# Fourth score column ahead of the second K, and a later copy of q, in a fused attention and mixture-of-experts kernel

## Chip, cores and metric

The kernel runs on one core of one Trainium2 chip. The metric is the device time of one launch in microseconds (us); lower is better. The time before is 945.1 us, the median of three runs (941.18 to 945.74).

## What is computed

Three layers follow one another. The attention has 8 batches, 8 heads, 576 rows and head size 64; K and V are first averaged over groups of 8 rows, so each head has 72 keys. Two layers of experts follow (4608 tokens of width 512, 8 experts, hidden width 1024). In the first, each token goes to the expert with the largest logit and is scaled by that expert's probability; the second does the same for tokens whose skip score is positive.

```python
k_p = k.reshape(B, H, Sp, 8, D).mean(axis=3); v_p = v.reshape(B, H, Sp, 8, D).mean(axis=3)
attn = softmax(scale * q @ k_p.T);  x = attn @ v_p          # [B*S, H*D] after a transpose
e = argmax(x @ w_gate + bias[modality]);  out[t] = p[t, e] * (relu(x[t] @ w1[e]) @ w2[e])
```

## The kernel before, in words

The order of instructions on each engine is written out by hand; each engine works through its own queue in that order, and a wait holds up all that stands behind it on the same queue. The attention goes through 36 *columns* of 128 query rows (all 8 heads at once), in the loop at L562, which runs to 39 because the product with V (`emit_AV`) trails the scores by LAG = 3 columns. A *unit* is 256 rows of one batch (two columns) or the last 64 rows of two batches (one column). Columns 0 to 3 belong to batch 0 and columns 4 to 7 to batch 1; column 8 has the rest of both. Columns 9 to 17, 18 to 26 and 27 to 35 are the next three pairs of batches.

One column goes through these steps:

- `split_q` (L156): ScalarE rearranges a loaded q unit; `emit_qT` (L283): TensorE transposes it into `ps_q`, ScalarE copies it out.
- `emit_S` (L305): eight matmuls against the pooled K (`KB`), VectorE takes the maximum (`mx`, L316); then VectorE runs what has been put off in the list `late` (L319), and five ticks of the background work are issued.
- `emit_exp` (L332): TensorE subtracts the maximum in PSUM (L336), ScalarE takes the exponential (L340). `ps_s` has one buffer, so the scores of a column wait for the exponential of the one before.
- `emit_eT` (L348) one column later, `emit_AV` (L366) three columns later, then VectorE divides by the sum (L395 to L402) and adds up the router's logits (L406).

K and V are pooled from raw loads by `pool_kb` (K of batches 0 and 1), `pool_k` (later K, in tiles of 108 rows) and `pool_v`, on GpSimd or VectorE as `pool_at` (L430) says; VectorE's share goes to `late` and so runs in the next column. `prep_kb`, `prep_k`, `prep_v1` and `prep_v2`, placed by `prep_at` (L441), transpose the pooled K and V on TensorE through the single PSUM buffer `ps_m` and copy them into `KB` and `VB`. All loads are issued on SyncE's queue: `next_q` (L481) loads q units in order, `next_kv` (L472) the K and V loads in the order of `order` (L462), each not before the column that frees its buffer.

Routing runs in the background while the attention goes on. `Background.tick` (L678) advances a generator by `pace` steps; each column has six ticks. `route` (L826) picks the expert of nine columns, counts tokens with a scan (L867), keeps the running count in `carry` (L871) and ranks tokens with two matmuls into `R` (L882, L883), which take `ps_m` as well. It is started after columns 12, 21 and 30 (`route_at`, L561); `lag` (L622) is the number of empty steps ahead of the second maximum (L850) and of the scan. `count` (L916) copies `carry` to `cb` (L919) and sums it by a matmul (L923); `early_pick` and `early_fill` call it with `copy=True`. `route_places` (L905) builds one-hot tiles `OB` on GpSimd. `early_slots` then names the tokens of the first blocks, which are gathered by GpSimd. `prepare_first` (L1488) splits the first expert's weights (`w1h`, `w1l`) and, at columns 32 and 33, transposes the first block's tokens through `ps_m` (`xT`, L1357), whose low half `xl` VectorE computes as a `late` item one column on.

The first block's products are mixed into the last columns; from about 210 us on the expert blocks run, a dense row of matmuls.

Of the kernel before, what the change touches and what calls it, by code (L numbers as in the profile page):

```python
# [55 lines left out]
def attention(tc, g, q, k, v, mid, w_gate, bias, const, moe):  # L56
# [3 lines left out]
    nc = tc.nc  # L60
    with ExitStack() as ctx:
# [28 lines left out]
        cols = []  # L90
# [9 lines left out]
        NC = len(cols)  # L100
# [322 lines left out]
        def idle():  # L423
            for _ in range(3):
# [5 lines left out]
        pool_at = {0: [(pool_kb, 1, 2, 4, P), (pool_kb, 1, 0, 2, V), (pool_kb, 1, 4, 5, V)],  # L430
                   1: [(pool_v, 1, 0, P)]}
# [5 lines left out]
        for b, cs in ((1, (3, 4, 4)), (2, (5, 6, 7)), (3, (10, 11, 12)), (4, (14, 15, 16)),  # L437
                      (5, (18, 19, 20)), (6, (20, 21, 22)), (7, (24, 25, 26))):
            for i, c in enumerate(cs):
                pool_at.setdefault(c, []).append((pool_v, b, 1, V, i, i + 1))  # L440
        prep_at = {1: [(prep_v1, 0)], 2: [(prep_kb, 1), (prep_v2, 0)],  # L441
                   5: [(prep_v1, 1)], 6: [(prep_v2, 1)], 7: [(prep_k, 0)],
                   8: [(prep_v1, 2, P)], 9: [(prep_v2, 2)], 11: [(prep_k, 1)],
                   13: [(prep_v1, 3, P)], 14: [(prep_v2, 3)],
                   17: [(prep_v1, 4)], 18: [(prep_v2, 4)], 20: [(prep_k, 2)],
                   21: [(prep_v1, 5)], 22: [(prep_v2, 5)], 24: [(prep_v1, 6)], 25: [(prep_k, 3)],
# [34 lines left out]
        def next_q(n):  # L481
            while n_q[0] < min(n, len(units)):
                load_q(n_q[0])
                n_q[0] += 1
# [77 lines left out]
        for c in range(NC + LAG):  # L562
            if c < NC:
                next_q(cols[c][0] + (5 if c > 1 else 4))
                next_kv(c)
                next_q(cols[c][0] + 5)
            bg.pace = {22: 2, 32: 1, 34: 2, 36: 3}.get(c, bg.pace)
            if 4 <= c < NC - 1:
                emit_S(c, lambda: emit_qT(c + 2))
            elif c < 4:  # L570
                if c > 0:
                    emit_S(c)
                    emit_eT(c - 1)
                    emit_exp(c)
                emit_qT(c + 2)
            elif c == NC - 1:
                emit_S(c)
                moe.gemm1_early()
# [11 lines left out]
            if c >= NC:  # L590
                for _ in av_t.pop(c - LAG - 1, ()):
                    pass
            emit_AV(c - LAG)
            if c == NC:
                emit_eT(c - 1)
                ks.close()
                moe.open_third()
            ahead = c + (3 if c < 2 else 4)
            if ahead < NC and cols[ahead][0] not in qs_t:
                split_q(cols[ahead][0])  # L600
# [19 lines left out]
            if c in route_at:  # L620
                c0, n = route_at[c]
                eng, lag = (nc.vector, (0, 0)) if c0 == 18 else (nc.gpsimd, (5, 8) if c0 == 0 else (4, 12))  # L622
# [44 lines left out]
class Background:  # L667


    def __init__(self):  # L670
        self.q = []
        self.hold = False
        self.pace = 1
# [152 lines left out]
def route(tc, g, r, lg, mask, c0, n, sp, pp, eng, wait=1, then=(), lag=(0, 0)):  # L826
# [30 lines left out]
    if n > 2:  # L857
# [13 lines left out]
        V.tensor_copy(r.carry, I[:, :, n - 1])  # L871
# [44 lines left out]
def count(tc, g, r, sp, pp, wait, copy=False):  # L916
    nc = tc.nc
    cb = sp.tile([128, E], BF16, tag="rc_cb", name="rc_cb", bufs=1)
    nc.vector.tensor_copy(cb, r.carry)  # L919
    for _ in range(wait):  # L920
        yield
    N = pp.tile([128, E], F32, tag="m", name="R")
    nc.tensor.matmul(N, lhsT=g.ones, rhs=cb, start=True, stop=True)  # L923
    if copy:
        ps, N = N, sp.tile([128, E], F32, tag="rc_N", name="rc_N", bufs=1)
        nc.scalar.copy(N, ps)
    else:
        g.bg.hold = True
    for _ in range(wait):
        yield  # L930
    return N
# [248 lines left out]
class Moe:  # L1180
# [307 lines left out]
    def prepare_first(self, c, sm, ps_q, ps_m, late):  # L1488
# [3 lines left out]
        if c in (32, 33):  # L1492
            self.g.bg.settle()
            self.xT(0, c - 32, ps_m.tile([128, 4, 128], F32, tag="m", name="ps_x"), late)
        if c == 36:
            self.gates1(0, sm)
# [598 lines left out]
```

## Time and profile before

| | us |
|---|---|
| median of three runs | 945.1 |
| the profiled execution | 943.7 |
| its span, first to last instruction | 941.9 |
| TensorE busy in the span | 893.1 (95%) |
| VectorE / ScalarE / GpSimd busy | 704.7 / 367.8 / 511.9 |

The profile is of one execution. A group of rows names the engine, the line of the kernel, the operation, the tile that is written and the tiles that are read; in a timeline a bracket gives how long the engine sat idle before the row and what released it. PEclk is the TensorE clock that was granted, as a share of 2.4 GHz.

### The profile page before, as it was taken

How to read it: one execution, taken by the hardware profiler on the slowest of the kernel's cores; microseconds unless marked ns; L12 is line 12 of the kernel's file. 1: busy time of each engine (PE TensorE's matmuls, PEld its weight loads, DVE VectorE, ACT ScalarE, POOL GpSimd, SP SyncE). 2: the span in 40 equal slices, each digit the busy share in tenths (PEclk: the TensorE clock that was granted, in tenths of full speed). 3: DMA queues.
4: the chain of work that ended last, by engine and by line, in shares of the span. 5: the costliest groups of instructions: out<-in, count | busy, mean ns of one | idle time of the engine just before them, and what ended most of it. 6: DMA issues, size and time to landing. Idle time of an engine off the chain costs nothing. (4 is left out here: it accounts for less than half of the span.)

```text
span 941.9 us, 19066 instructions
## 1 busy us (share of the span) xinstructions
PE 893.1 (95%) x6231; PEld 803.2 (85%) x6231; DVE 704.7 (75%) x1816; ACT 367.8 (39%) x727; POOL 511.9 (54%) x762
## 2 busy tenths in 40 slices
PE   7899989899999999998999989999999999999995
PEld 6799889888899999987999869999888988979993
DVE  5467886787777888889877898777665777688663
ACT  3466656453222222251222422213413556565551
POOL 5766797303246647666766556575653443445442
PEclk9999999999999999999999999999989999999998
DMA  9999965513212211441224521227115673671341
GB/s 233 216 255 264 256 195 157 193 62 121 69 58 86 74 38 64 143 153 66 83 83 130 172 79 64 75 72 253 58 65 156 206 230 126 202 244 36 111 161 44
DMA packets 86141, 126.07 MB, mean 134 GB/s; under 512 B 13192, under 2 KB 50104, under 8 KB 85866
## 3 DMA queue, kind: packets, MB, share of 16 engines
q1 hardware_dynamic: 75386, 96.68, 33.4%
q0 software_dynamic: 10608, 27.67, 9.7%
q8 instruction: 63, 1.03, 0.5%
q14 instruction: 84, 0.69, 0.2%
HBM read 182.09 MB, written 39.50 MB: 235 GB/s over the span
## 5 line engine op out<-in xcount | busy, mean ns | idle before, releaser
L1413 PE MATMUL ps_g<-xh,w1h 128*128 128x256 f32 x896 | 256.4, 286 | 2.5 <-DVE o L1652 1.5
L1413 PE MATMUL ps_g<-xl,w1h 128*128 128x256 f32 x896 | 253.3, 283 | 2.2 <-DVE xl L1366 2.2
L1413 PE MATMUL ps_g<-xh,w1l 128*128 128x256 f32 x896 | 252.7, 282 | 0.0
L1743 DVE CUSTOM_DVE_ANT_0 hr<-x,W 128x512 bf16<-128x512 f32 x324 | 228.1, 704 | 19.1 <-DVEq L1342 6.3
L1462 PE MATMUL ps_g<-w2h,hh 128*128 128x512 f32 x464 | 190.6, 411 | 3.0 <-ACT w2h L1353 1.6
L1462 PE MATMUL ps_g<-w2h,hl 128*128 128x512 f32 x464 | 185.4, 400 | 6.2 <-DVE hl L1418 6.1
L1462 PE MATMUL ps_g<-w2l,hh 128*128 128x512 f32 x464 | 184.6, 398 | 0.0
L1413 PEld LDWEIGHTS ps_g<-xh,w1h 128*128 128x128 f32 x896 | 169.7, 189 | 7.2 <-issue 2.3
L1413 PEld LDWEIGHTS ps_g<-xl,w1h 128*128 128x128 f32 x896 | 169.2, 189 | 4.0 <-DVE xl L1366 3.0
L1413 PEld LDWEIGHTS ps_g<-xh,w1l 128*128 128x128 f32 x896 | 169.5, 189 | 0.0
L1417 ACT ACTIVATE hh<-ps_g 128x512 fp32r<-128x512 f32 (+1 forms) x116 | 67.7, 584 | 248.8 <-PE ps_g L1413 246.6
L1418 DVE SCALAR_TENSOR_TENSOR hl<-ps_g,hh 128x512 fp32r<-128x512 f32 (+1 forms) x116 | 77.5, 668 | 64.1 <-ACT hh L1417 40.0
L911 POOL TENSOR_SCALAR OB<-iota,BB,pay 128x128 bf16<-128x128 bf16 x126 | 111.7, 894 | 21.5 <-DVE BB L899 21.4
L1462 PEld LDWEIGHTS ps_g<-w2h,hl 128*128 128x128 f32 x464 | 88.2, 190 | 29.5 <-DVE hl L1418 7.7
L1462 PEld LDWEIGHTS ps_g<-w2h,hh 128*128 128x128 f32 x464 | 88.6, 191 | 21.4 <-issue 2.5
L1462 PEld LDWEIGHTS ps_g<-w2l,hh 128*128 128x128 f32 x464 | 88.5, 191 | 16.7
L1354 DVE TENSOR_TENSOR w2l<-w2r,w2h 128x512 fp32r<-128x512 f32 x112 | 75.3, 710 | 6.6 <-ACT w2h L1353 4.6
L1333 POOL TENSOR_TENSOR w1l<-w1r,w1h 128x512 fp32r<-128x512 f32 x35 | 45.3, 1314 | 59.7 <-ACT w1h L1330 59.4
L1709 POOL DMA_INDIRECT out_dram<-x,dsi x38 | 47.6, 1252 | 44.5 <-DMA out_dram<-x,dsi 16.8
L1353 ACT CAST w2h<-w2r 128x512 fp32r<-128x512 f32 x112 | 63.9, 617 | 0.0
L1330 ACT CAST w1h<-w1r 128x512 fp32r<-128x512 f32 x112 | 63.7, 620 | 0.5 <-ACT hh L1417 0.5
L1323 POOL DMA_INDIRECT xg<-xd,gidx x38 | 44.1, 1162 | 33.7 <-DVE rs_lo L1174 16.5
(298 smaller groups left out, 1399.9 us busy)
## 6 DMA issues: line engine op xcount, KB each, us to landing
w1r<-in_moe_w_dram SPq DMA_DIRECT2D x128, 512.0 KB
w2r<-in_moe_w_dram SPq DMA_DIRECT2D x124, 512.0 KB
x2s<-x SPq DMA_DIRECT2D x19, 522.0 KB
v<-in_v_dram SPq DMA_DIRECT2D x48, 192.0 KB
xd<-x SPq DMA_DIRECT2D x16, 520.0 KB
q_sb<-in_q_dram SPq DMA_DIRECT2D x16, 512.0 KB
kt<-in_k_dram SPq DMA_DIRECT2D x32, 144.0 KB
x2s<-OBx SPq DMA_DIRECT2D x16, 261.0 KB
```

Of the source, the lines that this page charges most:

```text
L911: e.tensor_scalar(g.ob(c)[:, i, :], g.iota, r.BB[:, c:c + 1], r.pay[:, i, c:c + 1], ALU.is_equal, ALU.mult)
L1323: self.nc.gpsimd.indirect_dma_start(out=self.xg[i % 2][:, t, 0:w], out_offset=None, in_=src, in_offset=bass.IndirectOffsetOnAxis(ap=gidx[: ...
L1330: self.nc.scalar.copy(self.w1h[f], raw)
L1333: low() if late is None else late.append(low)
L1353: self.nc.scalar.copy(self.w2h[f], raw)
L1354: (eng or self.nc.vector).tensor_tensor(self.w2l[f], raw, self.w2h[f].bitcast(F32), ALU.subtract)
L1413: nc.tensor.matmul(out, lhsT=a[f][:, k, :], rhs=b[:, k, :], start=(n == 0), stop=(n == 11))
L1417: nc.scalar.activation(out=hh, in_=whole, func=ACTF.Relu)
L1418: nc.vector.scalar_tensor_tensor(hl, in0=whole, scalar=0.0, in1=hh.bitcast(F32), op0=ALU.max, op1=ALU.subtract)
L1462: nc.tensor.matmul(ps, lhsT=a[f][:, tt], rhs=b[f], start=(n == 0), stop=(n == 23))
L1709: self.nc.gpsimd.indirect_dma_start(out=self.out, out_offset=bass.IndirectOffsetOnAxis(ap=self.dsi[i % 2][:, t:t + 1], axis=0), in_=self.x ...
L1743: self.nc.vector.tensor_tensor_reduce(out=self.junk, in0=self.x2[i % 2][:, t, 0:DM], in1=self.W9[:, e, :], scale=1.0, scalar=0.0, op0=ALU. ...
```

## The change

The second K's last pooled part goes to column 1, its transposes (`prep_kb(1)`) from column 2 to the end of column 3's exponential, so that the scores of column 3 are issued ahead of it. `prep_v2(0)` moves forward between column 2's `emit_eT` and `emit_exp`. The first loads of q are interleaved one by one with the K and V loads, and `split_q` runs three columns ahead throughout. The V of batch 2 (the third) is pooled by VectorE and prepared one column later. `prep_k(3)` moves from column 25 to column 26. In the routing, the empty steps before the scans shrink from (5, 8) to (5, 1) and change from (4, 12) to (6, 3), the carry is copied on the engine of that route (GpSimd for the first two), `cb` is copied by ScalarE where `copy` is set, the pace rises and falls one column earlier, and the last early count waits, by `shut`, until column 35.

```diff
-        pool_at = {0: [(pool_kb, 1, 2, 4, P), (pool_kb, 1, 0, 2, V), (pool_kb, 1, 4, 5, V)],
-                   1: [(pool_v, 1, 0, P)]}
+        pool_at = {0: [(pool_kb, 1, 2, 4, P), (pool_kb, 1, 0, 2, V)],
+                   1: [(pool_v, 1, 0, P), (pool_kb, 1, 4, 5, V)]}
...
-        for b, cs in ((1, (3, 4, 4)), (2, (5, 6, 7)), (3, (10, 11, 12)), (4, (14, 15, 16)),
+        for b, cs in ((1, (3, 4, 4)), (2, (6, 7, 8)), (3, (10, 11, 12)), (4, (14, 15, 16)),
...
-        prep_at = {1: [(prep_v1, 0)], 2: [(prep_kb, 1), (prep_v2, 0)],
+        prep_at = {1: [(prep_v1, 0)],
                    5: [(prep_v1, 1)], 6: [(prep_v2, 1)], 7: [(prep_k, 0)],
-                   8: [(prep_v1, 2, P)], 9: [(prep_v2, 2)], 11: [(prep_k, 1)],
+                   9: [(prep_v1, 2, P)], 10: [(prep_v2, 2)], 11: [(prep_k, 1)],
...
-                   21: [(prep_v1, 5)], 22: [(prep_v2, 5)], 24: [(prep_v1, 6)], 25: [(prep_k, 3)],
+                   21: [(prep_v1, 5)], 22: [(prep_v2, 5)], 24: [(prep_v1, 6)],
...
         for c in range(NC + LAG):
-            if c < NC:
-                next_q(cols[c][0] + (5 if c > 1 else 4))
+            if c == 0:
+                for n in (4, 5, 6):
+                    next_q(n)
+                    next_kv(0, 1)
+                next_kv(0)
+            elif c == 2:
                 next_kv(c)
+                next_q(7)
+            elif c < NC:
                 next_q(cols[c][0] + 5)
-            bg.pace = {22: 2, 32: 1, 34: 2, 36: 3}.get(c, bg.pace)
+                next_kv(c)
+            bg.pace = {22: 2, 31: 1, 33: 2, 36: 3}.get(c, bg.pace)
+            if c == 35:
+                bg.shut = False
...
-            elif c < 4:
+            elif c < 2:
                 if c > 0:
                     emit_S(c)
                     emit_eT(c - 1)
                     emit_exp(c)
                 emit_qT(c + 2)
+            elif c == 2:
+                emit_S(c)
+                emit_eT(c - 1)
+                prep_v2(0)
+                emit_exp(c)
+                split_q(2)
+            elif c == 3:
+                emit_S(c)
+                emit_eT(c - 1)
+                emit_qT(4)
+                emit_exp(c)
+                prep_kb(1)
...
+            if c == 26:
+                prep_k(3)
             emit_AV(c - LAG)
+            if c == 3:
+                emit_qT(5)
...
-            ahead = c + (3 if c < 2 else 4)
-            if ahead < NC and cols[ahead][0] not in qs_t:
+            ahead = c + 3
+            if ahead < NC and c > 2 and cols[ahead][0] not in qs_t:
...
-                eng, lag = (nc.vector, (0, 0)) if c0 == 18 else (nc.gpsimd, (5, 8) if c0 == 0 else (4, 12))
+                eng, lag = (nc.vector, (0, 0)) if c0 == 18 else (nc.gpsimd, (5, 1) if c0 == 0 else (6, 3))
...
-        self.hold = False
+        self.hold = self.shut = False
...
-        V.tensor_copy(r.carry, I[:, :, n - 1])
+        eng.tensor_copy(r.carry, I[:, :, n - 1])
...
 def count(tc, g, r, sp, pp, wait, copy=False):
...
-    nc.vector.tensor_copy(cb, r.carry)
+    (nc.scalar.copy if copy else nc.vector.tensor_copy)(cb, r.carry)
     for _ in range(wait):
+        yield
+    while g.bg.shut:
         yield
...
             self.xT(0, c - 32, ps_m.tile([128, 4, 128], F32, tag="m", name="ps_x"), late)
+            self.g.bg.shut = True
```

## Rows read from the trace of the kernel before

**Rows 1.** Busy by stretch: us, PE, PEld, DVE, ACT, POOL, PEclk, DMA, GB/s.

```profile
30.00:40.00 10.00, 8.43 (x56) 8.02 (x56) 2.80 (x8) 3.89 (x10) 5.00 (x5) 0.83 0.83 210
...
60.00:70.00 10.00, 10.00 (x88) 9.98 (x86) 8.28 (x23) 6.96 (x15) 8.41 (x6) 1.00 1.07 298
...
330.00:353.00 23.00, 23.00 (x152) 20.74 (x151) 18.54 (x57) 4.67 (x9) 11.08 (x25) 1.00 0.08 29
```

**Rows 2.** Timeline of TensorE, columns 2 to 8: start us, us, engine, line, operation.

```profile
21.42 1.17 PE L310 MATMUL ps_s<-KB,qt 128*128 128x144 f32 x8
...
26.65 0.27 PE L217 MATMUL ps_k<-ident,kb 126*64 126x126 f32 x1
...
28.88 0.29 PE L222 MATMUL ps_k<-ident,kb 72*64 72x72 f32 x2
31.57 1.07 PE L274 MATMUL ps_g<-WGV,vt 128*96 128x32 f32 x6 [2.40 <-ACT KB L231]
32.45 2.27 PE L310 MATMUL ps_s<-KB,qt 128*128 128x144 f32 x8
...
37.85 1.14 PE L310 MATMUL ps_s<-KB,qt 128*128 128x144 f32 x8
...
41.88 1.14 PE L310 MATMUL ps_s<-KB,qt 128*128 128x144 f32 x8
...
52.22 2.29 PE L310 MATMUL ps_s<-KB,qt 128*128 128x144 f32 x8 [1.03 <-ACT ec L340]
...
58.25 1.20 PE L310 MATMUL ps_s<-KB,qt 128*64 128x144 f32 x16
```

**Rows 3.** Timeline of ScalarE: copies of q that waited, and an exponential.

```profile
27.00 0.65 ACT L340 ACTIVATE ec<-ps_s 128x576 f32<-128x576 f32 x1
...
29.66 1.04 ACT L167 COPY qs<-q_sb 128x1024 f32<-128x1024 f32 x1 [1.54 <-DMA q_sb<-in_q_dram]
...
49.10 1.05 ACT L167 COPY qs<-q_sb 128x1024 f32<-128x1024 f32 x1 [2.66 <-DMA q_sb<-in_q_dram]
```

**Rows 4.** Timeline of VectorE: maximum, V's pooling, the routing and its waits.

```profile
23.50 0.75 DVE L316 TENSOR_REDUCE mx<-ps_s 128x8 fp32r<-128x576 f32 x1
...
49.64 1.06 DVE L176 TENSOR_REDUCE v<-v 96x64 f32<-96x512 f32 x1 [0.66 <-DMA v<-in_v_dram]
...
95.04 2.37 DVE L867 TENSOR_TENSOR_SCAN rt_i<-within,rt_ms 128x72 bf16<-128x72 f32 x1
...
121.52 0.94 DVE L260 TENSOR_TENSOR VB<-v,half 96x768 f32<-96x768 f32 x1
...
129.00 0.23 DVE L850 TENSOR_REDUCE rt_my<-rt_eq 128x9 f32<-128x72 f32 x1 [1.90 <-POOL rt_eq L844]
...
169.72 0.31 DVE L867 TENSOR_TENSOR_SCAN rt_i<-within,rt_ms 128x72 bf16<-128x72 f32 x1
```

**Rows 5.** Timeline of GpSimd: K's pooling at the scan, and the one-hot tiles.

```profile
94.88 2.36 POOL L181 TENSOR_TENSOR t<-kt 108x1024 f32<-108x1024 f32 x1
...
120.91 6.86 POOL L911 TENSOR_SCALAR OB<-iota,BB,pay 128x128 bf16<-128x128 bf16 x8
```

**Rows 6.** Timeline of TensorE, columns 17 to 35.

```profile
100.50 0.51 PE L336 MATMUL ps_s<-mx,nident 128*128 128x288 f32 x2 [1.93 <-DVE mx L316]
...
119.64 1.17 PE L310 MATMUL ps_s<-KB,qt 128*128 128x144 f32 x8
...
140.36 0.40 PE L239 MATMUL ps_k<-ident,k 108*128 108x108 f32 x2 [1.62 <-POOL k L183]
...
146.88 1.23 PE L310 MATMUL ps_s<-KB,qt 128*128 128x144 f32 x8
...
164.83 1.23 PE L310 MATMUL ps_s<-KB,qt 128*128 128x144 f32 x8
...
182.01 0.19 PE L923 MATMUL R<-rc_cb,ones 128*128 128x8 bf16 x1 [2.18 <-DVE xl L320]
...
186.15 1.20 PE L310 MATMUL ps_s<-KB,qt 128*64 128x144 f32 x16
```

## Prediction

> **What bounds the kernel now.** I read the table of busy time by stretch first. The expert blocks after 210 us keep TensorE busy for all of their time at full clock, with the DMA engines nearly idle [rows 1], and the change touches nothing there: what the attention loses or saves passes one to one to the end. Second, TensorE's timeline through the attention. It runs through the columns at about 4.0 us each (37.85 to 41.88 [rows 2]) except where a wait opens a gap, so the question is which gaps close and which new ones open. A gap can cost more than itself: behind the 2.40 us before 31.57 the scores of column 3 took 2.27 us where column 4's took 1.14, and column 7's, behind 1.03 us of idle, took 2.29 [rows 2]. The granted clock of the stretch from 30 to 40 is 0.83 [rows 1], that is, part of it at 1.2 in place of 2.4 GHz. Third, the timelines of ScalarE, VectorE and GpSimd at each gap, to see what the releaser itself waited for.
>
> **Columns 2 to 8: minus 7.8 us.** Before, ScalarE stands until 29.66 for the q of columns 6 and 7 [rows 3]. The copies of the second K into `KB` are queued behind that wait, and TensorE stands 2.40 us for them; column 3, which needs neither, starts its scores at 32.45 [rows 2]. After the change column 3 needs only column 2's exponential. Column 2's scores, at 21.42 for 1.17 [rows 2], end at 22.6; with the last part of K out of the way the maximum (0.75 [rows 4]) follows at once and not at 23.50, then the subtraction (0.51 [rows 6]) and the exponential (0.65 [rows 3]); with some 0.4 for hand-overs column 3 starts at about 25.1. From there to column 4's scores TensorE does one column (4.0), the second K's transposes (26.65 to 29.17, 2.5 [rows 2]) and one more transpose of q (0.5): 32.1, not 37.85. `KB` is filled beside the product with V. The q of columns 6 and 7 is copied only after that, so column 4 gets 0.9 on top of its 4.0, and column 5 starts at 37.0, not 41.88.
> The next wait, ScalarE for q until 49.10 [rows 3], delayed column 6's exponential and so column 7's scores. It goes: that copy is issued a column later and its load ahead of half a K tile. Columns 5 and 6 with their prep matmuls take 8.7, so column 7 starts at 45.7, not 52.22; its half-clock stretch goes too, and with 4.0 and the transposes of `prep_k(0)` column 8 starts at 50.4, not 58.25. I keep 6 and 8 as bounds. `prep_v2(0)` and `prep_v1(2)` cost nothing more: the same matmuls at another place.
>
> **The loads: plus 1.5 us.** On SyncE's queue a unit of q now passes each of three K loads. Up to the third batch's V the bytes are the same, so I expect that V at 49.64 as before [rows 4]; VectorE asks for it at about 47.7 (column 7) and stands 1.9 us, of which its slack leaves some 0.3 on TensorE. The DMA engines are busy all through 60 to 70 us [rows 1], so the later loads can't come much sooner either, while their readers come eight microseconds sooner, less the one column of 4.0 by which the copies of q now come later. Waits like the one of 2.66 [rows 3] are possible, or none. I take 1.5 in all, bounds 0 and 3.
>
> **Columns 12 to 18: minus 2.2 us.** The first route's scan started at 95.04, just as GpSimd had begun a 2.36 us step of K's pooling [rows 5], and took 2.37; the same scan takes 0.31 at 169.72 [rows 4]. Column 17's maximum came late by it, and TensorE stood 1.93 us [rows 6]. Seven steps fewer put the scan into column 15, ahead of the pooling, and the carry goes to GpSimd. I add 0.3 for the slower columns around it. Bounds 1 and 2.2.
> The one-hot tiles now start a column earlier and run beside VectorE's scaling of V. VectorE's scaling at 121.52 took 0.94 us [rows 4] in the midst of eight one-hot steps of 6.86 us together [rows 5]: no delay, so I charge none. The Trainium skill, "SBUF — State Buffer", section "SBUF: two separate sides", has VectorE's instructions with two SBUF inputs and GpSimd's reads share a port under an exclusive lock held for a whole instruction. By that rule such a scaling would wait for the one-hot step in flight, up to 0.9 us, and the gain would be that much smaller where TensorE waits; the scan at 95.04 agrees with the rule, the scaling at 121.52 doesn't.
>
> **Columns 22 to 27: minus 1.4 us.** Column 22's scores to column 27's took 27.2 us (119.64 to 146.88 [rows 6]), against an estimated 21.4 without waits (five columns at 4.0 and 1.4 of prep matmuls). VectorE stood 1.90 us for GpSimd [rows 4], which was behind with one-hot tiles, and TensorE 1.62 us for K's pooling [rows 6]. These 5.8 us go with the earlier route and `prep_k(3)` a column later. New waits take their place. At pace 2 the six empty steps fall between two VectorE instructions of one column, 22, so the second maximum still waits for GpSimd and column 23's maximum is about 1.0 us late. In column 23 the copy to `cb` stands in ScalarE's queue ahead of that column's copies and exponential; it waits for GpSimd's carry, which waits for VectorE's scan, itself behind the maximum, V's third part and the logits. Column 24's scores, which need that exponential, come 1.7 us late. In column 25 the ranking falls together with the scaling of V and a third of V's pooling, some 6 us of VectorE's work in a 4 us column: 1.7 us on column 26, near the 1.93 of [rows 6]. Together 4.4 new against 5.8 old. Bounds: minus 5.8 (all hidden) and plus 2 (new half-clock stretches).
>
> **Columns 31 to 35: minus 2.1 us.** They took 21.3 us (164.83 to 186.15 [rows 6]). The count's matmul stood 2.18 us for `xl`, as VectorE still had to read `ps_m`, and a half-clock stretch followed. With `shut` it comes in column 35, free of both (3.5); the lower pace of column 31 gives 1.0. But by my count of ticks the ranking matmuls move from column 32 to column 33, behind the first `xT`, where `ps_m` is held by column 33's `xl`: the same wait in another place, about 1.7. Net 2.8, less 0.7 for the chance of a half-clock stretch. Bounds 0.3 and 3.5.
>
> **The tail: 0.** The last early count comes three of its own steps later, so its gather goes out about one early product (1.9 us) later, which is about its readers' slack. Bounds minus 0.5 and plus 1.5. `cb` on ScalarE costs nothing there: its carry is old by then.
>
> **Sum.** -7.8 + 1.5 - 2.2 - 1.4 - 2.1 = -12.0 us. The profiled execution's 943.7 (span 941.9 and 1.8 around it) would become 931.7; it lies 1.4 below the median of 945.1, so a median of the new kernel should be about 933.
>
> **The rivals.**
> *The loads take it back.* For it: the DMA share of 1.07 [rows 1]; against: no engine stands for a load of q or V after 49.64 [rows 3, 4]. Each load comes when it came before, and the columns gain only the closed half-clock stretches and the routing: about 7 us, 938.
> *The routing's new waits eat what they free.* Columns 22 to 35 give nothing or lose 2: 936.5 to 939. The ticks I counted speak for it; against, that K's pooling no longer meets the scan.
> *Nothing shows.* Columns 2 to 8 gain 4, the loads cost 3, the rest cancels but for 1: about 943.
> *Slower: GpSimd's pooling of K becomes the bound.* TensorE has stood for it before (1.62 [rows 6]). If the next K tile is not pooled when column 11 ends, at about 67, every later column waits for it, one to one. The 0.75 MB of q put ahead of K is 3.6 us at the 210 GB/s of [rows 1]; it decides once K is over 12 us late, which takes a blocked queue as well: 948 to 952.
> That an edit doesn't do what it says I see only for `cb` of the last count of all, where `copy` is not set and VectorE keeps it; nothing hangs on that.
>
> **How the numbers follow.** Forecast 0.58; loads 0.16; routing 0.15; nothing 0.07; slower 0.04. About 0.5% (4.7 us) is what a measurement of this kernel can tell from no change, so faster means below 940.4: the forecast, the loads and the routing lie there but for their upper ends: 0.82. Same 0.14, slower 0.04. The range takes in the bounds of the terms, not all their extremes together: 927.5 to 940.0.
>
> **What would show it.** Right: column 3's scores near 25 us, column 4's near 32, column 8's near 50, and a granted clock near 1 from 30 to 40 us; a scan of 0.3 us in column 15 and no gap at column 17; the count's matmul without a wait in column 35. New gaps should stand at column 24's scores (ScalarE), column 26's subtraction (VectorE) and column 33's ranking matmuls (`xl`). Wrong: ScalarE waiting for q or GpSimd for K for over 3 us in columns 9 to 13, or column 27's scores less than 7 us ahead of before. The expert blocks must keep their length; if they don't, the base of the sum is wrong.

## The result, and the profile of the changed kernel

The changed kernel takes 951.1 us (median of 7 runs, 946.72 to 951.8) where the kernel before took 941.39 beside it (7 runs): ratio 1.0087, 95% interval 1.0066 to 1.0108. It is slower by 0.9%; the forecast had 933. The profiled execution took 950.15 us, its span is 948.5. The two profiled executions lie 6.5 us apart (943.7 and 950.15), the medians 9.7: the rows below account for the 6.5. One run of a repetition below took 3095 us and is left out of its ratio.

Read first the scores of the first columns in TensorE's timeline of the changed kernel; they answer to [rows 2]. A bracket gives the idle time ahead of the row and what ended it.

```profile
22.57 1.17 PE L310 MATMUL ps_s<-KB,qt 128*128 128x144 f32 x8
25.96 1.25 PE L310 MATMUL ps_s<-KB,qt 128*128 128x144 f32 x8 [0.79 <-ACT ec L340]
33.09 1.15 PE L310 MATMUL ps_s<-KB,qt 128*128 128x144 f32 x8
...
51.91 1.20 PE L310 MATMUL ps_s<-KB,qt 128*64 128x144 f32 x16
```

Column 3 starts at 25.96 in place of 32.45, column 8 at 51.91 in place of 58.25, although this execution's first scores came 0.93 us later. Then the waits of TensorE behind column 8, in the same timeline:

```profile
63.78 0.51 PE L336 MATMUL ps_s<-mx,nident 128*128 128x288 f32 x2 [1.30 <-DVE mx L316]
67.87 0.66 PE L289 MATMUL ps_q<-ident,qs 128*128 128x128 f32 x4 [0.56 <-ACT qs L167]
...
108.67 0.66 PE L289 MATMUL ps_q<-ident,qs 128*128 128x128 f32 x4 [2.72 <-ACT qs L167]
119.03 0.66 PE L289 MATMUL ps_q<-ident,qs 128*128 128x128 f32 x4 [1.51 <-ACT qs L167]
125.16 0.51 PE L336 MATMUL ps_s<-mx,nident 128*128 128x288 f32 x2 [0.46 <-DVE mx L316]
128.38 1.25 PE L310 MATMUL ps_s<-KB,qt 128*128 128x144 f32 x8 [1.21 <-ACT ec L340]
142.33 0.85 PE L336 MATMUL ps_s<-mx,nident 128*128 128x288 f32 x2 [3.19 <-DVE mx L316]
...
178.71 0.21 PE L907 MATMUL R<-M,trim 128*128 128x72 bf16 x1 [1.61 <-DVE xl L320]
207.04 1.58 PE L1058 MATMUL W<-er_oa,OB 128*128 128x2 bf16 x54 [3.16 <-DVE er_oa L1043]
```

The waits of 1.93 and 2.18 us of [rows 6] are gone. The new ones stand in four places: behind VectorE in column 10, behind the copy of q in columns 20 and 22, behind VectorE and ScalarE in columns 23 to 26, and behind `er_oa` among the first block's products. The bracket names the last releaser only. In column 20 the copy itself stood 3.02 us for its load; in column 22 ScalarE stood 1.86 us for VectorE ahead of the copy, and VectorE, in its own timeline, for a load of V:

```profile
116.47 1.04 DVE L176 TENSOR_REDUCE v<-v 96x64 f32<-96x512 f32 x1 [1.33 <-DMA v<-in_v_dram]
```

The table of busy time by stretch, with the columns of [rows 1], shows the clock around them:

```profile
30.00:40.00 10.00, 9.36 (x75) 8.59 (x74) 5.05 (x13) 5.30 (x13) 3.25 (x4) 1.00 0.82 191
60.00:70.00 10.00, 8.13 (x73) 7.52 (x72) 9.49 (x19) 5.04 (x10) 9.69 (x8) 1.00 1.03 303
100.00:110.00 10.00, 7.17 (x60) 6.71 (x59) 7.13 (x17) 4.15 (x9) 9.69 (x11) 1.00 0.97 292
...
140.00:150.00 10.00, 7.67 (x34) 7.65 (x35) 5.81 (x19) 3.31 (x9) 9.89 (x13) 0.56 0.48 119
200.00:210.00 10.00, 6.84 (x97) 6.45 (x94) 7.35 (x24) 3.48 (x11) 0.00 (x0) 0.81 0.25 80
210.00:220.00 10.00, 8.40 (x39) 6.89 (x39) 6.82 (x24) 6.34 (x7) 2.26 (x4) 0.85 0.19 53
```

From 30 to 40 the granted clock is now 1.00 (0.83 in [rows 1]). But behind the 3.19 us of idle in column 26 it falls to 0.56 from 140 to 150, and behind the 3.16 us at `W` to 0.81 and 0.85 from 200 to 220: parts of these stretches at 1.2 in place of 2.4 GHz. Behind the 2.72 us in column 20 it stays 1.00 (100 to 110).

Set against the trace of before, start by start, the changed kernel's lead comes and goes so (scores' start to scores' start; the last step is from column 35's scores, 186.15 before and 185.65 after, to the first block's second product, 210.72 and 214.52):

| stretch | before | after | difference | forecast |
|---|---|---|---|---|
| columns 0 to 8 | 44.95 | 37.68 | -7.3 | -7.8 |
| 8 to 13 | 21.08 | 23.38 | +2.3 | part of +1.5 |
| 13 to 18 | 23.26 | 20.92 | -2.3 | -2.2 |
| 18 to 23 | 21.37 | 26.17 | +4.8 | part of +1.5 |
| 23 to 28 | 26.85 | 31.00 | +4.1 | -1.4 |
| 28 to 35 | 35.34 | 32.27 | -3.1 | -2.1 |
| tail | 24.57 | 28.87 | +4.3 | 0 |

With the 0.9 us of the start that is +3.8 at the second product; from 240 to 420 us it is +4.4. The last 2.2 us of the span come later, behind gaps between passes of the experts that both kernels have: from 440 to 445 us the changed kernel's clock is 0.50, where the kernel before had 0.71 in the same place (435 to 440).

### The profile page after: what moved, and what is told of

The parts are those of the page before. It is cut to its first block, busy times and chain, and to the rows that moved or that the text cites. A ratio compares the mean times of both kernels' runs of the same rounds, so it can differ in the third digit from the quotient of the medians.

```text
span 948.5 us, 19064 instructions
## 1 busy us (share of the span) xinstructions
PE 894.1 (94%) x6231; PEld 804.3 (85%) x6231; DVE 703.7 (74%) x1811; ACT 369.0 (39%) x730; POOL 507.8 (54%) x764
## 5 line engine op out<-in xcount | busy, mean ns | idle before, releaser
L936 POOL TENSOR_SCALAR OB<-iota,BB,pay 128x128 bf16<-128x128 bf16 x126 | 107.4, 861 | 15.4 <-DVE BB L924 15.3
L1550 ACT ACTIVATE x<-ps_g,gate 128x512 f32<-128x512 f32 x37 | 25.6, 691 | 96.6 <-PE ps_g L1489 85.6
```

Of the source, the lines that this page charges most:

```text
L936: e.tensor_scalar(g.ob(c)[:, i, :], g.iota, r.BB[:, c:c + 1], r.pay[:, i, c:c + 1], ALU.is_equal, ALU.mult)
L1550: nc.scalar.activation(out=self.x2[i % 2][:, t, 0:DM], in_=ps, func=ACTF.Copy, scale=self.gate[i % 2][:, t:t + 1])
```

## Experiments

A ratio is against the kernel before, in the same rounds on the same chip; the bracket behind it is its 95% interval. A diff is against the kernel named and shows of a line only the piece that changes.

**Which part loses? The three parts one by one.** `early_only` is the changed kernel with routing and last part put back; `routing_only` and `tail_only` are the kernel before with one part.

```diff
# early_only, against the changed kernel
-            bg.pace = {22: 2, 31: 1, 33: 2, 36: 3}.get(c, bg.pace)
+            bg.pace = {22: 2, 32: 1, 34: 2, 36: 3}.get(c, bg.pace)
-            if c == 35:
-                bg.shut = False
-            if c == 26:
-                prep_k(3)
+  24: [(prep_v1, 6)], 25: [(prep_k, 3)],
-  (5, 1) if c0 == 0 else (6, 3)
+  (5, 8) if c0 == 0 else (4, 12)
-        eng.tensor_copy(r.carry, I[:, :, n - 1])
+        V.tensor_copy(r.carry, I[:, :, n - 1])
-    (nc.scalar.copy if copy else nc.vector.tensor_copy)(cb, r.carry)
+    nc.vector.tensor_copy(cb, r.carry)
-    while g.bg.shut:
-        yield
-            self.g.bg.shut = True
# routing_only, against the kernel before: the lags, eng for carry, nc.scalar.copy for cb, prep_k(3)
# tail_only, against the kernel before: the paces and bg.shut
```

> The kernel before with only the attention's early part: column 3 ahead of the second K, the new order of the q loads, the copy of q three columns ahead to the end, the third V a column later. Routing, counts and paces as before. Theory A (the loads are the clock until about column 23: each lands when it landed before, so a lead won in column 3 is spent waiting for q): column 3's scores near 26 us, a lead of 4 us left in column 13, with the 1.9 us wait of column 17 back in place, and at column 23's scores no more than 2 us ahead of before; at the end minus 2 to plus 1 us on the kernel before. Rival B (the lead of 6 us is carried to the end, and what was lost is lost in the routing alone): column 23's scores near 118 us and minus 5 to minus 6 us at the end.

> The kernel before with only the routing's part: the empty steps of the first two routes, the carry on the route's engine, the early counts' copy by ScalarE, prep_k(3) in column 26. Theory A: column 17's wait of 1.9 us goes, but column 24's scores wait about 1.2 us for ScalarE and column 26's subtraction 3 us for VectorE's maximum, with a half-clock stretch behind it, so that column 28's scores come 1 to 3 us later than before; plus 1 to plus 3 us at the end. Rival B, the forecast's sum for these columns: column 28's scores 3.6 us earlier, minus 3 to minus 4 us at the end.

> The kernel before with only the last part: pace up and down one column earlier, the last early count held back until column 35. Theory A: columns 31 to 35 gain about 2.8 us, then the matmuls of W stand 3.2 us for er_oa in front of the seventh early product, half-clock products follow, and the second product of the first block starts 28.9 us after column 35's scores in place of 24.6: 1 to 2 us slower than before. Rival B (the tail's loss is a passing half-clock stretch): minus 2 to minus 3 us. Rival C (forecast): minus 2.1 us with a tail of 24.6 us.

Measured: early part 940.39 us, ratio 0.9977 (0.9955 to 1.0000); routing 950.92, 1.0090 (1.0064 to 1.0116); last part 945.87, 1.0027 (1.0006 to 1.0049). The three differences add up to 0.94%, about the whole change's 0.87%. So the early part doesn't lose; the routing does, and the last part a little.

In the trace of the early part alone column 3 starts at 24.36, the lead is 5.8 us in column 13, 4.8 in column 23 and 6.2 at the second product: there rival B was right. At the end it is 3.3, and the median gains 2.6. In the routing's trace columns 23 to 28 take 34.3 us (26.85 before); the largest wait comes from the second maximum (`rt_my`) on VectorE:

```profile
128.17 0.23 DVE L852 TENSOR_REDUCE rt_my<-rt_eq 128x9 f32<-128x72 f32 x1 [3.76 <-POOL rt_eq L846]
```

Those 3.76 us answer to the 1.90 of [rows 4]; but here column 23's maximum is queued behind it, and TensorE's subtraction stands 4.65 us for that maximum (0.46 in the changed kernel's trace, 2.58 in its repetition); column 26's stands 2.29. In the last part's trace columns 31 to 35 gain 2.8 us, `W` stands 3.15, and the tail takes 28.3 us: theory A.

**Is the early lead the rule?** `early_again` is the same kernel once more.

> The early part alone a second time, for how far its lead at column 23 and after column 35 (5 and 6 us in the first trace) is the rule, when the median gained only 2.6 us. Theory A, weakened (the lead is at the mercy of the loads): in another execution the lead at column 13 differs by several us, and the median lies again 1 to 4 us below that of before. Rival B (the lead is always there, and is lost to TensorE's clock between the expert blocks): column 13 again near minus 5.8 us, and the loss after 427 us again.

940.38 us, ratio 0.9968 (0.9945 to 0.9990): the median repeats. The trace doesn't: the lead is 4.1 us in column 13 (its first scores came 1.2 us later than in the first trace) and gone at column 23. Behind column 17's wait of 1.92 us the product with V took 3.08 us, and 1.66 behind the same wait in the first trace; in column 22 TensorE stood 2.30 us for the copy of q, which stood behind VectorE's 2.14 us for a load of V. So the early part is worth 2.7 us here, and how much of its lead an execution keeps depends on the loads, theory A's weakened form, and on the clock behind a wait.

**Is the wait for q the lost column of slack, or the loads?** `early_q4` copies q four columns ahead again; `after_k8` takes a K load out of the way.

```diff
# early_q4, against early_only
-            ahead = c + 3
+            ahead = c + (3 if c < 9 else 4)
# after_k8, against the changed kernel: the order of the K and V loads
-  ("v", 11), ("k", 8), ("v", 12), ("v", 13), ("k", 9)
+  ("v", 11), ("v", 12), ("k", 8), ("v", 13), ("k", 9)
```

> The same as the kernel before, but from column 9 on q is copied four columns ahead, as before the change. If the waits of TensorE for the copy of q (0.56, 2.72 and 1.51 us in the changed kernel, at 67.87, 108.67 and 119.03) come from the lost column of slack, they go, and column 23's scores come some 3 to 4 us earlier than with three columns ahead; time 2 to 4 us less. If the landing of the loads alone decides, the copy asks a column earlier and ScalarE stands longer with other work behind it: within 1 us of three ahead, or slower.

> The changed kernel with one load moved: the first half of the last K tile (pooled in column 23) is issued behind the V of batch 6, in column 18, and so behind two q units that it stood in front of. Theory (TensorE's waits for the copy of q in columns 20 to 23, 2.72 and 1.51 us, are the loads' order: 0.9 MB of K that is needed later is in front of q): the first of them goes, the q load is issued some 5 us earlier than at 101.44 us; column 22's scores come 2 to 3 us earlier than in the changed kernel, of which the routing's waits behind it may keep a part: 1 to 3 us less, 948 to 950. Rival (the DMA engines carry all they can, whatever the order): the wait moves to another load, less than 1 us.

`early_q4`: 943.49 us, ratio 1.0010 (0.9991 to 1.0030): the early gain is gone. ScalarE's and then TensorE's timeline show where:

```profile
65.37 1.04 ACT L167 COPY qs<-q_sb 128x1024 f32<-128x1024 f32 x1 [6.67 <-DMA q_sb<-in_q_dram]
```

```profile
66.77 0.85 PE L274 MATMUL ps_g<-WGV,vt 128*96 128x32 f32 x6 [1.77 <-ACT vt L259]
68.49 2.29 PE L310 MATMUL ps_s<-KB,qt 128*128 128x144 f32 x8 [0.88 <-ACT ec L340]
```

The copy asks a column earlier, finds its load not landed, and `vt` and the exponential wait behind it; half-clock scores (2.29 us) follow. Here the landing decides, and three columns ahead is right. For columns 20 to 23 it settles nothing: this trace came there without a lead and had no wait.
`after_k8`: 950.89 us, ratio 1.0076 (1.0059 to 1.0092), no gain. The waits of 2.72 and 1.51 are gone, and one of 5.71 stands at 119.56. TensorE's timeline names the copy of q; the copy stood behind VectorE, and VectorE, in the second timeline, for a load of V that is behind the moved K load in both orders. It landed no sooner than before (117.03, and 116.47 in the changed kernel), while its reader came sooner:

```profile
119.56 1.12 PE L289 MATMUL ps_q<-ident,qs 128*128 128x128 f32 x4 [5.71 <-ACT qs L167]
```

```profile
117.03 1.02 DVE L176 TENSOR_REDUCE v<-v 96x64 f32<-96x512 f32 x1 [5.55 <-DMA v<-in_v_dram]
```

The rival's outcome was right: the wait moved to another load. Its reason isn't shown: from 100 to 110 and from 110 to 120 us the DMA share was 0.97 and 0.92 in the changed kernel, and 0.98 and 0.80 with the other order. Whether the bytes or a load's place in SyncE's queue sets its landing stays open.

**What in the routing loses? First the first route.** `early_scan` gives the early part the first route's short lag, with the carry left on VectorE; `early_r1` also puts that carry on GpSimd. In both the second route is held where it stood.

```diff
# both, against early_only
-  (5, 8) if c0 == 0 else (4, 12)
+  (5, 1) if c0 == 0 else (11, 12)
# early_scan: prep_k(3) in column 26 as well
# early_r1
-        V.tensor_copy(r.carry, I[:, :, n - 1])
+        (V if c0 == 9 else eng).tensor_copy(r.carry, I[:, :, n - 1])
```

> The early part, the first route's lag (5, 1), and prep_k(3) in column 26; the second route's lag is (11, 12), that is, seven steps more for the seven fewer of the first, so that its second maximum, scan and ranking stand where they stood before; carry and cb by VectorE, counts and paces as before. Theory (the routing's loss is the place of the second route on VectorE and ScalarE's queues alone): column 17's 1.9 us and the 1.6 us for K's pooling in column 26 go and nothing new comes in columns 23 to 28: 2 to 3.5 us less than the early part alone, 936 to 938. Rival (the earlier one-hot tiles on GpSimd are the loss): new waits for GpSimd or VectorE in columns 23 to 27 again, no gain or a loss.

> The early part with the first route's lag (5, 1) and its carry on GpSimd; the second route stands where it did (lag (11, 12), carry and cb by VectorE), prep_k(3) in column 25. Theory (carry on GpSimd keeps K's pooling behind the scan): the scan takes 0.3 us in place of the 1.67 us that it took with the carry on VectorE, the carry 0.2 in place of 1.18, and column 18's scores have 2 us more of a lead than column 16's; columns 23 to 28 lose nothing; 938 to 939 us. Rival (the waits for q behind column 20 take it back): column 23 no further ahead than in the early part alone, 940.

`early_scan`: 942.9 us, ratio 1.0007 (0.9989 to 1.0026); columns 13 to 18 took 24.5 us, more than before (23.3). VectorE's rows of its scan and carry, and GpSimd's of the same time:

```profile
86.53 1.67 DVE L890 TENSOR_TENSOR_SCAN rt_i<-within,rt_ms 128x72 bf16<-128x72 f32 x1
88.23 1.18 DVE L894 CAST carry<-rt_i 128x8 f32<-128x8 bf16 x1
```

```profile
85.64 2.39 POOL L181 TENSOR_TENSOR t<-kt 108x1024 f32<-108x1024 f32 x1
88.11 1.27 POOL L182 TENSOR_TENSOR t<-t 108x512 f32<-108x512 f32 x1
```

The scan ends at 88.20, GpSimd's step at 88.03; the carry, 8 elements a lane, ends at 89.41, GpSimd's next step at 89.38. And `prep_k(3)` in column 26 met the second route's `R` in `ps_m` (2.26 us for `rt_rk`), a new wait that the theory had not named.
`early_r1`: 940.9 us, ratio 0.9966 (0.9946 to 0.9986); columns 13 to 18 took 20.9 us, as in the changed kernel, where these rows of VectorE and GpSimd stand:

```profile
87.14 0.29 DVE L892 TENSOR_TENSOR_SCAN rt_i<-within,rt_ms 128x72 bf16<-128x72 f32 x1
```

```profile
87.50 0.19 POOL L896 CAST carry<-rt_i 128x8 f32<-128x8 bf16 x1 [1.33 <-DMA kt<-in_k_dram]
87.85 2.37 POOL L181 TENSOR_TENSOR t<-kt 108x1024 f32<-108x1024 f32 x1 [0.15 <-DMA kt<-in_k_dram]
```

With the carry in its own queue GpSimd starts K's pooling behind the scan. The first route's edits do what they were forecast to do; but the median is no better than the early part's, because columns 20 to 23 took 15.4 us in place of 13.1, with 1.91 us of waiting for the copy of q behind VectorE's 1.75 for a load of V: the rival, by another load than it named.

**Then the second route.** `after_r2old` puts it back in the changed kernel (lag (11, 12), carry and `cb` by VectorE). `r2_cb` puts back the copies alone, `r2_rank` the ranking's place alone, both on the changed kernel with the repaired tail (`after_tail5`, below).

```diff
# after_r2old, against the changed kernel
-  (5, 1) if c0 == 0 else (6, 3)
+  (5, 1) if c0 == 0 else (11, 12)
-        eng.tensor_copy(r.carry, I[:, :, n - 1])
+        V.tensor_copy(r.carry, I[:, :, n - 1])
-    (nc.scalar.copy if copy else nc.vector.tensor_copy)(cb, r.carry)
+    nc.vector.tensor_copy(cb, r.carry)
# r2_cb, against after_tail5: the last edit, and (V if c0 == 9 else eng) for the carry
# r2_rank, against after_tail5: prep_k(3) in column 25, and ahead of R
-    for _ in range(4 if wait else 1):
+    for _ in range((16 if lag[0] == 6 else 4) if wait else 1):
```

> The changed kernel, with the second route alone put back: lag (11, 12), carry and cb by VectorE; the later counts' cb is by VectorE too. Theory: the waits at column 24's scores (1.21 us for ScalarE) and column 26's subtraction (3.19 us for VectorE's maximum) go with the half-clock stretch behind the second; column 28's scores come 4 to 5 us earlier than in the changed kernel, 945 to 947 us. Rival (VectorE is overloaded in columns 24 to 27 whatever the order): column 28 less than 2 us earlier.

> The changed kernel with the repaired tail, and with the second route's carry and the early counts' cb by VectorE as before the change; the lag stays (6, 3). Theory (the larger part of the second route's loss is its place, which puts the ranking beside V's scaling on VectorE in column 25): the 1.2 us of column 24's scores for ScalarE goes, column 26's subtraction still stands about 3 us for VectorE's maximum; within 2 us of the changed kernel with the repaired tail, 942 to 945. Rival (the copy on ScalarE is the loss): column 26's wait shrinks as well, 4 us less, 940.

> The changed kernel with the repaired tail, the second route's ranking twelve steps (one column) later, and prep_k(3) in column 25; the copy of cb stays on ScalarE. Theory (place): column 24's 1.2 us stays, column 26's wait for the maximum falls below 1 us and the half-clock stretch behind it goes; column 28's scores stand 4 us better against column 23's than in the changed kernel: 939 to 941 us. Rival (the copy on ScalarE): no better than the repaired tail alone, 944.

`after_r2old`: 946.11 us, ratio 1.0022 (1.0001 to 1.0043), 5 us less than the changed kernel, as the theory had it in time. Its trace is of its slowest execution (952.76), and column 28's scores don't come earlier there: the scan's 1.7 us gap in column 16 is back (its carry was on VectorE), columns 13 to 18 take 26.1 us in place of 20.9, and `prep_k(3)` waits 2.26 us, as in `early_scan`. The waits of 1.21 and 3.19 are gone.
`r2_cb`: 941.21 us, ratio 0.9982 (0.9966 to 0.9998). Column 24's wait for ScalarE is gone, column 26's still 2.35; columns 23 to 28 took 29.2 us, against 31.4 with the repaired tail alone.
`r2_rank`: 938.49 us, ratio 0.9941 (0.9914 to 0.9968); columns 23 to 28 took 24.8 us. Its waits there:

```profile
127.24 0.51 PE L336 MATMUL ps_s<-mx,nident 128*128 128x288 f32 x2 [0.42 <-DVE mx L316]
130.48 1.25 PE L310 MATMUL ps_s<-KB,qt 128*128 128x144 f32 x8 [1.23 <-ACT ec L340]
142.30 0.19 PE L905 MATMUL R<-M,trim 128*128 128x72 bf16 x1 [1.49 <-ACT KB L244]
```

ScalarE's 1.23 stays, VectorE's 3.19 is gone. So the place of the ranking (with that of `prep_k(3)`) is worth 6.6 us of these columns and the copies 2.2. VectorE's timeline of column 25 in the changed kernel shows why:

```profile
133.81 0.76 DVE L316 TENSOR_REDUCE mx<-ps_s 128x8 fp32r<-128x576 f32 x1
134.48 1.37 DVE L260 TENSOR_TENSOR VB<-v,half 96x768 f32<-96x768 f32 x1
135.78 1.03 DVE L176 TENSOR_REDUCE v<-v 96x64 f32<-96x512 f32 x1
136.75 0.13 DVE L992 TENSOR_SCALAR first<-er_mx 128x1 int32<-128x1 f32 x1
136.81 1.45 DVE L993 TENSOR_SCALAR star<-desc,er_mx 128x8 f32<-128x8 f32 x1
...
138.50 0.21 DVE L916 TENSOR_TENSOR rt_rk<-M,R 128x72 f32<-128x72 bf16 x1
...
140.12 0.32 DVE L1034 TENSOR_TENSOR er_am<-M,star 128x144 f32<-128x144 bf16 x1
...
141.53 0.75 DVE L316 TENSOR_REDUCE mx<-ps_s 128x8 fp32r<-128x576 f32 x1
```

From one maximum to the next its rows fill 7.7 us of a column of 4: the scaling, V's third, `star`, seven steps of ranking, and the division. Not all of it is work: `star`, 8 elements a lane, takes 1.45 where it took 0.21 in the kernel before (at 144.43), and the scaling 1.37 in place of 0.94; the last section shows beside what.

**The tail.** `after_p35` brings the last count's steps forward by a higher pace; `after_tail5` also puts `W` three steps later, so that `er_oa` and `W` stand in their old places on VectorE and TensorE.

```diff
# both, against the changed kernel
-            bg.pace = {22: 2, 31: 1, 33: 2, 36: 3}.get(c, bg.pace)
+            bg.pace = {22: 2, 31: 1, 33: 2, 35: 3}.get(c, bg.pace)
# after_tail5 also, in early_slots
-    yield
-    yield
+    for _ in range(5 if C == 27 else 2):
+        yield
```

> The changed kernel with pace 3 in column 35 in place of 2, so that the last early count, held back to column 35, reaches er_oa and W two early products sooner. Theory (the tail's loss is that count's lateness): W's matmuls don't stand for er_oa, no half-clock stretch at 208 to 214 us, and from column 35's scores to the first block's second product it takes 24.6 us in place of 28.9: 3 to 4.5 us less than the changed kernel, 947 us. Rival (VectorE is full there, and any place of er_oa makes TensorE wait): the wait moves to another product, less than 1 us.

> The changed kernel with pace 3 in column 35 and three more empty steps ahead of W of the second early gather, which puts er_oa back to right behind the fourth early product's hl on VectorE, and W behind the last column's product with V and the fifth early product, as before the change. Theory (W stands because only one early product lies between er_oa and W, with that product's hl and w2l ahead of er_oa on VectorE): no wait of W, 24.6 us from column 35's scores to the first block's second product in place of 28.9; 3.5 to 4.5 us less than the changed kernel, 947 us. Rival (the tail is short of VectorE's time): W waits over 1 us again.

`after_p35`: 949.88 us, ratio 1.0077 (1.0046 to 1.0108), against the theory. `er_oa` was in its old place, but `W` now came ahead of the last column's product with V, and waited again (the tail took 29.3 us):

```profile
200.41 1.58 PE L1058 MATMUL W<-er_oa,OB 128*128 128x2 bf16 x54 [3.23 <-DVE er_oa L1043]
```

`after_tail5`: 944.07 us, ratio 0.9996 (0.9978 to 1.0014); no wait of `W`, and 24.4 us for the tail. Since the medians lay 7 us apart and the traces 4.5, both ran once more side by side:

> The changed kernel once more, on the same chip and in the same rounds as the next one, for the size of the tail's loss: a ratio between 1.006 and 1.010 and, in the trace, 28.5 to 29.5 us from column 35's scores to the first block's second product, with W standing about 3.2 us.

> The changed kernel with the repaired tail once more. If the tail's loss is only what its trace shows (4.5 us), 4 to 5 us less than the changed kernel beside it; if a later loss hangs on the order in the tail, 7 us or more, as the two medians of different chips had it (951.1 and 944.1).

The changed kernel 950.68, ratio 1.0080 (1.0054 to 1.0106); with the repaired tail 944.2, ratio 1.0021 (0.9998 to 1.0045); the tails took 28.9 and 24.4 us. 6.5 us apart in the medians, and by the intervals anything from 2 to 9, which has room for the 4.5 that the traces show. `er_oa` and `W` with the repaired tail, on VectorE and TensorE, from the second of its executions:

```profile
200.23 0.40 DVE L1445 SCALAR_TENSOR_TENSOR hl<-ps_g,hh 128x256 fp32r<-128x256 f32 x1
200.55 0.20 DVE L1043 TENSOR_TENSOR er_oa<-iota_a,er_a 128x54 bf16<-128x54 f32 x1
```

```profile
200.81 1.49 PE L1058 MATMUL W<-er_oa,OB 128*128 128x2 bf16 x54
```

and VectorE in the changed kernel:

```profile
205.67 0.43 DVE L1445 SCALAR_TENSOR_TENSOR hl<-ps_g,hh 128x256 fp32r<-128x256 f32 x1 [0.55 <-ACT hh L1444]
206.17 0.69 DVE L1381 TENSOR_TENSOR w2l<-w2r,w2h 128x512 fp32r<-128x512 f32 x1
206.78 0.21 DVE L1043 TENSOR_TENSOR er_oa<-iota_a,er_a 128x54 bf16<-128x54 f32 x1
```

There the fifth product's `hl` and `w2l` are queued ahead of `er_oa`, and `W` behind the sixth product: TensorE reaches `W` 3.16 us too soon.

**What gains, put together.** `early_tail5` is `early_only` with the paces, `bg.shut` and the repair of `after_tail5`; `early_r1_tail5` is `early_r1` with the same.

> The early part and the last part with the same repair of the tail; the first two routes as before the change. Theory: the parts add: minus 2.7 us for the early part and minus 2.8 us for columns 31 to 35, without the tail's loss: 937 to 938 us, ratio 0.994. Rival (TensorE's clock at the first product is what counts, and the lead is lost elsewhere): no better than the early part alone, 940.

> The early part, the first route's lag (5, 1) with its carry on GpSimd, the second route where it stood, and the last part with the repaired tail. If the parts add: the early part and the first route 940.9 (ratio 0.9966), the last part 2.8 us less: 937 to 938, ratio 0.993, no worse than the early and last parts alone (0.9938). Rival (the first route's gain is taken back by waits for q near column 21): as the early and last parts alone or 1 us slower.

`early_tail5`: 937.6 us, ratio 0.9938 (0.9917 to 0.9958); `early_r1_tail5`: 939.65, ratio 0.9960 (0.9938 to 0.9983). The early and the last part add; the first route brings nothing more, since columns 20 to 23 took 18.9 us with it (3.63 of it waiting for a load of q) and 13.5 without. With `r2_rank` there are two versions 0.6% faster than the kernel before and some 1.4% faster than the changed one.

## Why the prediction was wrong, step by step

- *Columns 2 to 8, -7.8*: right. Column 3 came at 25.96 (25.1 forecast, with terms that add up to 24.9), column 4 at 33.09 (32.1), the clock of 30 to 40 us was 1.00, and the fifteen traces with the early part and q three ahead gained 5.9 to 9.3 us on the one trace of before (44.95 us for columns 0 to 8; the two other traces without the early part took 43.2 and 44.2).
- *"No engine stands for a load of q or V after 49.64"; the loads, +1.5*: failed. The 2.3 us of columns 8 to 13 are not the loads': they are the same in fourteen of those fifteen traces. By the rows, VectorE's token arithmetic of columns 9 and 10 stands longer beside GpSimd's pooling of K (below): three instructions took 4.9 us in all, and 2.2 before, where they met the pooling too. V's third, which the change puts ahead of them in column 9, is part of the same stretch; no run separates the two. The loads took 4.5 us in columns 20 to 23 (2.72 for q, 1.51 for V), where I had looked for waits up to column 13 only: what is not in the way before is not thereby slack. The rival "the loads take it back" named the mechanism, at a smaller price.
- *Columns 12 to 18, -2.2*: right in size (-2.3). The reason was not the one given: the shorter lag alone left the scan beside the pooling (`early_scan`); the carry on GpSimd, which the step only mentioned, holds the pooling back.
- *Columns 22 to 27, -1.4*: failed, the step that decided most: +4.1 from column 23 to 28, +6.4 in the second trace. The three waits stood where I had put them, and in the first trace their sum was near: 0.46 in column 23 (1.0 forecast), 1.21 in column 24 (1.7), 3.19 in column 26 (1.7), 4.9 against 4.4. What the sum left out is the half-clock stretch behind the last, which I had in the bound alone: the product with V at 143.69 took 3.16 us, eight microseconds later 1.66, and the rows from 142.33 to 151.55 some 4.4 us more than such rows take at full clock (an estimate from the rows of before). And column 26's price set VectorE's standing at nothing. "Some 6 us of VectorE's work in a 4 us column" was right as work; some 1.7 us more went by beside GpSimd's pooling. Without them, by the same rows, the wait would have been about 1.5; no run tests that.
- *Columns 31 to 35, -2.1*: right, -2.8; the count without a wait, the ranking 1.61 us for `xl` (1.7 forecast).
- *The tail, 0*: failed, +4.3. I counted how much later the gather would be, and not what TensorE would meet: a matmul placed in its queue one product behind the VectorE step that it reads. The bound of +1.5 was for the gather.
- *"What the attention saves passes one to one to the end"*: failed in part. The table of [rows 1] shows the expert blocks from 330 to 353 us; from 430 to 435 the kernel before has TensorE busy for 2.39 of 5 us, and from 435 to 440 the clock at 0.71. Set against the trace of before, the lead shrinks from the second product to the end by up to 5.2 us (`after_r2old`) and in no trace grows by more than 0.2, with the clock behind the gaps between passes. Whether the early part loses half of its lead there as a rule, or had less of it in most executions than in its first trace, isn't settled: only two of its executions have a trace.

## What to carry to other kernels

When work put into idle steps between engines is moved, price it by the queue that it lands in: write down for each moved instruction what stands ahead of it on its engine and how many instructions of the reader lie between, as the last 3 us at `W` hung on one product of distance. The time won where an early stall closes can go again at a later load: look for the next reader of a load, however far on, and follow a bracket to the engine that stands for the load itself. And a wait of TensorE can cost as much again: a slow stretch came behind 3.19 us in column 26 and none behind 2.72 in column 20, and the same 1.92 us in column 17 had one in one execution and none in another. Such a stretch belongs into the sum with its chance, not into the tail of the range alone.

## What the hardware showed that I had not expected

VectorE's smallest instructions took as long as GpSimd's pooling step beside them. From VectorE's and GpSimd's timelines of the changed kernel, columns 9 and 10:

```profile
59.37 1.05 DVE L838 TENSOR_SCALAR ti<-tm,qf 128x4 int32<-128x4 f32 x1
60.67 1.14 DVE L843 CAST pay<-th 128x36 f32<-128x36 int32 x1
...
63.64 2.71 DVE L847 CAST pay<-ti 128x36 f32<-128x36 int32 x1
```

```profile
58.03 2.36 POOL L181 TENSOR_TENSOR t<-kt 108x1024 f32<-108x1024 f32 x1
60.47 1.30 POOL L182 TENSOR_TENSOR t<-t 108x512 f32<-108x512 f32 x1
...
63.96 2.35 POOL L181 TENSOR_TENSOR t<-kt 108x1024 f32<-108x1024 f32 x1
```

The ends agree: 60.42 and 60.39, 61.81 and 61.77, 66.35 and 66.31. Four to 36 elements a lane, some 0.2 us of work (`th`, between them, took 0.18), stand until GpSimd's step is over; so did `star` (138.26, GpSimd's step on V 138.22), and already the scan of [rows 4] (97.41) beside the pooling of [rows 5] (97.24). It goes the other way too: while VectorE scaled V from 134.48 to 135.85, GpSimd's last pooling step of K took 1.32 us, and 0.72 elsewhere.

The trace of before had it on V's scaling too. In VectorE's timeline, beside a pooling step that ended at 137.56, the scaling took twice the 0.94 of [rows 4]:

```profile
136.41 1.96 DVE L260 TENSOR_TENSOR VB<-v,half 96x768 f32<-96x768 f32 x1
```

With the one-hot tiles of [rows 5] it is GpSimd that stands. The scaling in their midst, from 121.52 to 122.46, was hardly held up (beside such steps it took 0.94 to 1.11 in all traces), but the step of GpSimd that started during it was; the next one shows what a step takes alone:

```profile
121.69 1.45 POOL L911 TENSOR_SCALAR OB<-iota,BB,pay 128x128 bf16<-128x128 bf16 x1
...
123.12 0.79 POOL L911 TENSOR_SCALAR OB<-iota,BB,pay 128x128 bf16<-128x128 bf16 x1
```

It ended 0.7 us after the scaling, and so did every one-hot step of these traces that started during a scaling.

The Trainium skill, "SBUF — State Buffer", section "SBUF: two separate sides", has the port that VectorE and GpSimd share as an exclusive lock for a whole instruction, against VectorE's instructions with two SBUF inputs or in a fast mode. The ends above agree with the lock for the scan and the scaling, which read two tiles; `ti`, `star` and the casts read one, and no run here shows in which mode they ran. In one point the traces differ from it: at 119.45 in the changed kernel the scaling took 0.94 although a one-hot step was under way until 119.91. The forecast set the rule aside for the row of 0.94, and read it wrongly: the one-hot step of 1.45 beside it agrees with the rule.

Priced by such rows as 1.96, the standing beside the pooling would have come into the sum for columns 9, 10 and 25.
